# One sixteenth of the output weights loaded by GpSimd in six row transfers, with ten 2-byte transfers between them, in a fused decode block (attention and MLP) on one core

## The chip, the cores and the metric

One Trainium2 chip, one of its cores. The metric is the device time of one execution in microseconds (us), as a median over executions. The kernel before takes 669.44 us (four executions, 669.28 to 669.69). None was over 1.5% above the fastest of its kernel, and all count as fast. Faster or slower are given at 2%, 13.4 us.

## The reference

Eight sequences decode one token each through an attention layer with a key and value cache, and a two-layer MLP, both with conditional layer norms. Cut to what matters here:

```python
B, Sq, D = (8, 1, 512);  Hq, Hkv, Sk, Dh = (32, 8, 8192, 128);  F = 1792
h = layernorm(x) * (1 + ca) + sa
q = (h @ wq)                                   # 32 heads
scores = einsum(q, k_cache) * Dh ** -0.5       # the cache: 2 x 8 x 8 x 8192 x 128 bf16
o = einsum(softmax(scores), v_cache)
x = x + ga * (o @ wo)                          # wo: 4096 x 512 bf16, 4 MB
h = layernorm(x) * (1 + cb) + sb
x = x + gb * (relu(h @ w1 + b1) ** 2 @ w2 + b2)
```

The cache is 268 MB, all inputs together 284 MB. Each byte is used once.

## The kernel before

SyncE issues nearly all loads into a ring of four slots of 4 MB. The tiles of this kernel have up to 128 rows, called partitions (`[128, ...]` in its code). The parts that matter are the output weights `wo`, loaded once near the start, and their first reader near the end.

```python
wo_sb = sb("wo_sb", [128, HQ, D], BF16)
...
load(0)                      # keys of the first two heads, 4 MB, 32 KB per partition
load(1)
d_b1 = dma("sync", s_bb, ...)
d_b2 = dma("sync", s_bb, ...)
d_wo = dma("sync", s_wo, lambda e: e.dma_start(
    wo_sb[:, :, :].rearrange("p (g j) n -> p g (j n)", j=4),
    A_wo.rearrange("(g p j) n -> p g (j n)", g=8, p=128)))   # 8 groups x 128 rows of 4 KB
load(2)                      # waits until the slot is free, as do all later loads
load(3)
...
# last batch: the first reader of wo (24 matmuls), then 32 more for groups 6 and 7
t = op("tensor", lambda e, g=g, j=j: e.matmul(bank(7)[32 * j:32 * (j + 1), :], ...,
       wo_sb[:, 4 * g + j, :], ...), [k_oP, d_wo])
...
# last of all: the second MLP weight, the output, the store
```

Of the kernel before, what the change touches and what calls it, by code (L numbers as in the profile page):

```python
# [9 lines left out]
BF16 = mybir.dt.bfloat16  # L10
# [23 lines left out]
class Prog:  # L34
# [19 lines left out]
    def op(self, eng, fn, deps=()):  # L54
        o = Op(eng, fn, deps, None, self.at)
        o.tok = Tok(o, self.at)
        self.ops[eng].append(o)
        return o.tok

    def dma(self, eng, sem, fn, deps=()):  # L60
        self.dma_n[sem] = self.dma_n.get(sem, 0) + 16
        self.ops[eng].append(Op(eng, fn, deps, sem, self.at))
        return Tok(None, self.at, sem, self.dma_n[sem])
# [105 lines left out]
def bass_adaLN_cond__gqa_block_cached__dense_activation_squared_relu__decode_kernel(  # L169
# [17 lines left out]
    with ExitStack() as es:  # L187
        E = es.enter_context
        sb = lambda name, shape, dt: E(nc.sbuf_tensor(name, shape, dt))
        RING = sb("ring", [128, NSLOT, UNIT], BF16)  # L190
        KTb = sb("KTb", [128, 2, 32, 128], BF16)
        wo_sb = sb("wo_sb", [128, HQ, D], BF16)
# [24 lines left out]
        ONE8 = sb("ONE8", [1, B], BF16)  # L217
        PERM = sb("PERM", [128, 4, 32], BF16)
        epst = sb("epst", [128, 1], FP32)
        stats = sb("stats", [B, 6], FP32)  # L220
        mv = sb("mv", [B, 2], FP32)
        std_ = sb("std_", [B, 1], FP32)
# [47 lines left out]
        Pg = Prog(nc, E)  # L270
        op, dma = Pg.op, Pg.dma
        sem = lambda name: E(nc.semaphore(name))
        s_c, s_x, s_wm, s_wq, s_wo, s_bb = (
            sem(f"d_{n}") for n in ("c", "x", "wm", "wq", "wo", "bb"))
        s_w1 = [sem(f"d_w1{i}") for i in range(2)]
        s_w2 = [sem(f"d_w2{i}") for i in range(4)]
        s_ring = [sem(f"d_r{i}") for i in range(NSLOT)]
# [63 lines left out]
        k_all = t  # L341
# [9 lines left out]
        def load(n):  # L351
            kv, b, p = units[n]
            s = n % NSLOT
            src = (A_k_cache if kv == "k" else A_v_cache)[b, 2 * p:2 * p + 2]
            src = src.rearrange("g s d -> (g s d)").rearrange("(p f) -> p f", p=128)
            dep = [released.get(s)]
            if units[n] == last:
                t0, toks = 0, []
                for i, t1 in enumerate(CH):
                    toks.append(dma("sync", s_last[i], lambda e, a=t0 * DH, z=t1 * DH: e.dma_start(  # L360
                        RING[:, s, a:z], src[:, a:z]), dep))
                    t0 = t1
                loaded[n] = toks
            else:
                loaded[n] = dma("sync", s_ring[s], lambda e: e.dma_start(slot(s), src), dep)
# [67 lines left out]
        for g in range(HKV):  # L433
            r0 = 16 * (g % 2) + 4 * (g // 2)
# [3 lines left out]
        def fcol(ap, f):  # L438
# [9 lines left out]
        load(1)  # L448
        d_b1 = dma("sync", s_bb, lambda e: e.dma_start(b1_row, B_b1.rearrange("(o f) -> o f", o=1)))
        d_b2 = dma("sync", s_bb, lambda e: e.dma_start(b2_row, B_b2.rearrange("(o f) -> o f", o=1)))  # L450
        d_wo = dma("sync", s_wo, lambda e: e.dma_start(
            wo_sb[:, :, :].rearrange("p (g j) n -> p g (j n)", j=4),
            A_wo.rearrange("(g p j) n -> p g (j n)", g=8, p=128)))
        load(2)
        load(3)
        next_load = NSLOT
# [53 lines left out]
        def permute(q0, q1, dst, deps):  # L510
            pP = bank(6)[:, 64 * q0:64 * q1].rearrange("p (g j b) -> p g j b", j=4, b=B)
            for hl in range(REP):
                for j in range(4):
                    t = op("tensor", lambda e, hl=hl, j=j: e.matmul(
                        pP[32 * hl:32 * (hl + 1), :, j, :].rearrange("p (q h) b -> p h q b", h=2),
                        PERM[:, j, :], oTn_p[:, :, q0:q1, hl, :], start=True, stop=True,
                        tile_position=(0, 32 * hl)), deps)
            return op("vector", lambda e: e.tensor_copy(dst, pP), [t])

        def project(k_oP):  # L520
            for g in range(6):
                for j in range(4):
                    t = op("tensor", lambda e, g=g, j=j: e.matmul(
                        bank(7)[32 * j:32 * (j + 1), :], oP[:, g, :, :].rearrange("p j b -> p (j b)"),
                        wo_sb[:, 4 * g + j, :], start=(g == 0), stop=(g == 5), tile_position=(0, 32 * j)),
                        [k_oP, d_wo])
            return op("vector", lambda e: e.tensor_copy(proj, bank(7)), [t])

        for b in range(B):
# [5 lines left out]
            for p in range(NP):  # L535
                n = 2 * NP * b + p
# [69 lines left out]
            for p in range(NP):  # L606
                if p == NP - 1:
                    Pg.at = "post" if lastb else (b, "b")
                n = 2 * NP * b + NP + p
# [3 lines left out]
                if not lastu:  # L613
# [30 lines left out]
                    if lastb and p == NP - 2:  # L644
                        Pg.at = "post"
                        k_proj = project(permute(0, 3, oP[:, 0:6], [norm_last, k_all] + stg_free + hold))
                        for k in range(KT):
                            op("tensor", lambda e, k=k: e.matmul(
                                yT_ps[:, k, :], b2_row[:, k * 128:(k + 1) * 128], ONE8[:, :],
                                start=(k == 0), stop=False, skip_group_check=True), [d_b2, s_bank_free[2]])  # L650
                else:
# [22 lines left out]
                    for m in range(28):  # L674
# [6 lines left out]
                        if m == 15:  # L681
                            for f in range(FT):
                                op("tensor", lambda e, f=f: e.matmul(
                                    hT_ps[f // 7][:, f % 7, 1, :], fcol(b1_row, f), ONE8[:, :],
                                    start=(f % 7 == 0), stop=False, skip_group_check=True), [d_b2, s_bank_free[f // 7]])
                            for k in range(KT):
                                op("tensor", lambda e, k=k: e.matmul(
                                    attn_ps[:, k, :], proj[:, 128 * k:128 * (k + 1)], SELP[:, :],
                                    start=(k == 0), stop=False, skip_group_check=True), [k_proj])
                    osb = O_sb[:, 1, :]  # L690
                    t = op("vector", lambda e: e.tensor_copy(osb, bank(3)), [t])
                    for i in range(4):
                        op("tensor", lambda e, i=i: e.matmul(
                            oT_ps, osb[:, i * 128:(i + 1) * 128], SEL[:, i, :], start=(i == 0), stop=False,
                            skip_group_check=True), [t, k_all])
# [4 lines left out]
                    k_oP = permute(3, 4, oP[:, 6:8], [t])  # L700
                    for g in (6, 7):
                        for j in range(4):
                            for k in range(KT):
                                k_attn = op("tensor", lambda e, g=g, j=j, k=k: e.matmul(
                                    attn_ps[:, k, :], wo_sb[:, 4 * g + j, k * 128:(k + 1) * 128], oP[:, g, j, :],
                                    start=False, stop=(g == 7 and j == 3), skip_group_check=True), [k_oP, d_wo])


        t = op("vector", lambda e: e.tensor_tensor(t1T[:], attn_ps, mod(2), ALU.mult), [k_attn])
# [2 lines left out]
        for k in range(KT):  # L712
            t = op("tensor", lambda e, k=k: e.matmul(mean_ps, ONESMB[:, :], x1T[:, k, :], start=(k == 0),
                                                    stop=(k == KT - 1)), [k_x1])
        o_ps = bank(4)[:, 0:256]
        for cc in range(2):
            for k in range(2):
                op("tensor", lambda e, k=k, cc=cc: e.matmul(
                    o_ps[64 * cc:64 * cc + B, 128 * k:128 * (k + 1)], x1T[:, 2 * cc + k, :], IDENT[:, :],
                    start=(k == 0), stop=False, tile_position=(0, 64 * cc), skip_group_check=True), [k_x1])  # L720
# [10 lines left out]
        for k in range(KT):  # L731
# [4 lines left out]
            for f in range(FT):  # L736
                t = op("tensor", lambda e, f=f, k=k: e.matmul(
                    hT_ps[f // 7][:, f % 7, :, :], wcol(k, f), hbT[:, k, :, :], start=False, stop=(k == KT - 1),
                    skip_group_check=True), [k_hb, k_sb, d_w1[k // (KT - 1)]])
# [9 lines left out]
        for f in range(FT):  # L749
            for k in range(KT):  # L750
                t = op("tensor", lambda e, f=f, k=k: e.matmul(
                    yT_ps[:, k, :], W2v[:, f, k * 128:(k + 1) * 128], hidT[:, f, :],
                    start=False, stop=(f == FT - 1), skip_group_check=True), [k_sq[f // 7], d_w2[f // 4]])
# [3 lines left out]
        for cc in (1, 0):  # L757
            for k in range(2):
                t = op("tensor", lambda e, k=k, cc=cc: e.matmul(
                    o_ps[64 * cc:64 * cc + B, 128 * k:128 * (k + 1)], y2T[:, 2 * cc + k, :], IDENT[:, :],  # L760
                    start=False, stop=(k == 1), tile_position=(0, 64 * cc), skip_group_check=True), [k_y2])
# [39 lines left out]
```

## Time and profile before

| what | value | view |
|---|---|---|
| time | 669.44 us | four executions |
| span of the profiled execution | 667.6 us | page |
| bytes read | 283.66 MB, 425 GB/s over the span | page |
| share of the DMA engines' time on SyncE's queue (q1) | 99.1% | page |
| TensorE busy | 513.8 us, 77% | page |
| chain that ended last | PE 52%, DMA 37% | page |

The chain names TensorE for half of the span, since each key load is released by the TensorE work that empties its slot (SyncE's own waits: 342.4 us for the matmuls of L496, 31 times, and 215.9 us for those of L630, 28 times). The queue table shows the stronger limit: the 16 DMA engines are at work nearly all the time, 99.1% of it for SyncE's queue. SyncE's own timeline shows how its loads are issued at the start (start, length, engine, line, operation, tile, count):

```profile
3.68 0.40 SPq L451 DMA_DIRECT2D wo_sb<-in_A_wo_dram  x1
14.59 23.87 SPq L365 DMA_DIRECT2D ring<-in_A_k_cache_dram  x2
```

The third and fourth key loads are entered from 14.59 on; the second of them is not accepted before 38.46 (14.59 + 23.87).

### The profile page before, as it was taken

How to read it: one execution, taken by the hardware profiler on the slowest of the kernel's cores; microseconds unless marked ns; L12 is line 12 of the kernel's file. 1: busy time of each engine (PE TensorE's matmuls, PEld its weight loads, DVE VectorE, ACT ScalarE, POOL GpSimd, SP SyncE). 2: the span in 40 equal slices, each digit the busy share in tenths (PEclk: the TensorE clock that was granted, in tenths of full speed). 3: DMA queues.
4: the chain of work that ended last, by engine and by line, in shares of the span. 5: the costliest groups of instructions: out<-in, count | busy, mean ns of one | idle time of the engine just before them, and what ended most of it. 6: DMA issues, size and time to landing. Idle time of an engine off the chain costs nothing.

```text
span 667.6 us, 15485 instructions
## 1 busy us (share of the span) xinstructions
PE 513.8 (77%) x7064; PEld 344.8 (52%) x7064; DVE 302.6 (45%) x571; ACT 258.7 (39%) x289; POOL 18.4 (3%) x76
## 2 busy tenths in 40 slices
PE   3493984898739985699848987499756998389885
PEld 2283731675328742577317853287425773177534
DVE  2262731566216651367314662166513673156722
ACT  2151640466105660266404662066502654046610
POOL 7300000000000000000000000000000000000000
PEclk9696997899969998699977999699987999779996
DMA  9999999999999999999999999999999999999996
GB/s 376 431 412 437 426 427 435 432 430 430 434 434 430 430 432 436 428 432 432 436 428 430 434 434 430 430 434 434 428 432 434 434 426 434 432 434 428 434 415 264
DMA packets 12176, 283.85 MB, mean 425 GB/s; under 512 B 1250, under 2 KB 1283, under 8 KB 3588
## 3 DMA queue, kind: packets, MB, share of 16 engines
q1 hardware_dynamic: 12116, 283.65, 99.1%
q8 instruction: 9, 0.15, 0.1%
q10 hardware_dynamic: 48, 0.02, 0.0%
q14 instruction: 3, 0.02, 0.0%
HBM read 283.66 MB, written 0.01 MB: 425 GB/s over the span
## 4 chain that ended last, share of the span: by engine, by line
PE 52%; DMA 37%; ACT 7%; DVE 2%; SPq 1%; issue 1%
PE PS L479 36%; DMA ring<-in_A_k_cache_dram 32%; PE PS L496 9%; ACT P_sb L562 5%; PE PS L616 2%; DMA ring<-in_B_w_dram 2%; DMA ring<-in_A_wq_dram 2%; PE PS L469 1%; SPq L659 1%; ACT KTb L484 1%; DVE O_sb L626 1%; PE PS L463 1%; PE PS L574 1%; DVE Pm L588 0%; PE PS L594 0%
## 5 line engine op out<-in xcount | busy, mean ns | idle before, releaser
L484 ACT ACTIVATE KTb<-PS 128x1024 bf16<-128x1024 bf16 x192 | 196.5, 1024 | 332.2 <-PE PS L479 332.2
L479 PE MATMUL PS<-IDENT,ring 128*128 128x128 bf16 x4096 | 267.4, 227 | 51.2 <-DMA ring<-in_A_k_cache_dram 51.2
L479 PEld LDWEIGHTS PS<-IDENT,ring 128*128 128x128 bf16 x4096 | 246.8, 102 | 99.6 <-DMA ring<-in_A_k_cache_dram 52.4
L486 DVE COPY KTb<-PS 128x1024 bf16<-128x1024 bf16 x320 | 210.1, 687 | 143.9 <-PE PS L479 141.8
L616 PE MATMUL PS<-ring,Pm 128*32 128x512 bf16 x992 | 70.4, 434 | 46.8 <-DMA ring<-in_A_v_cache_dram 45.9
L496 PE MATMUL PS<-KTb,Qb 128*32 128x512 bf16 x1024 | 78.8, 385 | 4.5 <-ACT KTb L484 4.5
L626 DVE CAST O_sb<-PS 128x512 bf16<-128x512 f32 x31 | 21.4, 692 | 126.7 <-PE PS L616 126.7
L616 PEld LDWEIGHTS PS<-ring,Pm 128*32 128x32 bf16 x992 | 26.8, 106 | 85.5 <-DMA ring<-in_A_v_cache_dram 54.4
L562 ACT ACTIVATE P_sb<-PS,negm 128x1024 bf16<-128x1024 f32 x32 | 35.2, 1112 | 20.2 <-DVE negm L557 20.2
L469 PE MATMUL PS<-ONES 128*128 128x512 f32 x80 | 42.1, 630 | 0.0
L574 PE MATMUL PS<-IDENT,P_sb 128*128 128x128 bf16 x256 | 19.9, 220 | 15.4 <-ACT P_sb L562 15.4
L588 DVE COPY Pm<-PS 64x512 bf16<-64x512 bf16 x48 | 20.2, 421 | 25.0 <-PE PS L574 24.5
L574 PEld LDWEIGHTS PS<-IDENT,P_sb 128*128 128x128 bf16 x256 | 14.4, 98 | 25.1 <-ACT P_sb L562 25.1
L463 PE MATMUL PS<-IDENT 128*128 128x512 bf16 x88 | 26.9, 380 | 0.0
L496 PEld LDWEIGHTS PS<-KTb,Qb 128*32 128x32 bf16 x1024 | 15.4, 94 | 21.1 <-ACT KTb L484 8.5
L503 DVE TENSOR_REDUCE m<-PS 128x1 f32<-128x512 f32 x32 | 22.0, 689 | 6.6 <-PE PS L496 6.6
L630 PEld LDWEIGHTS PS<-SEL,O_sb 128*128 128x128 bf16 x124 | 5.8, 97 | 30.5 <-DVE O_sb L626 30.5
L469 PEld LDWEIGHTS PS<-ONES 128*128 128x128 f32 x80 | 12.7, 190 | 10.6 <-issue 10.6
L630 PE MATMUL PS<-SEL,O_sb 128*128 128x8 bf16 x124 | 7.9, 169 | 12.4 <-DVE O_sb L626 12.0
L641 DVE TENSOR_TENSOR oTn<-PS,rinv 128x8 f32 x31 | 6.0, 194 | 14.9 <-PE PS L630 14.9
L463 PEld LDWEIGHTS PS<-IDENT 128*128 128x128 bf16 x88 | 7.7, 105 | 9.1 <-issue 7.2
L484 ACT ACT_TABLE_LOAD x8 | 10.3, 1283 | 3.2 <-issue 3.2
(132 smaller groups left out, 115.9 us busy)
## 6 DMA issues: line engine op xcount, KB each, us to landing
ring<-in_A_k_cache_dram SPq DMA_DIRECT2D x32, 4096.0 KB, 34.2
ring<-in_A_v_cache_dram SPq DMA_DIRECT2D x31, 4096.0 KB, 27.8
ring<-in_A_wq_dram SPq DMA_DIRECT2D x1, 4096.0 KB, 19.9
wo_sb<-in_A_wo_dram SPq DMA_DIRECT2D x1, 4096.0 KB, 47.6
ring<-in_w_mod_dram SPq DMA_DIRECT2D x1, 3072.0 KB, 10.3
ring<-in_A_v_cache_dram SPq DMA_DIRECT2D x1, 2048.0 KB, 22.6
ring<-in_B_w_dram SPq DMA_DIRECT2D x3, 512.0 KB, 19.4
ring<-in_B_w_dram SPq DMA_DIRECT2D x1, 1344.0 KB, 17.9
```

The source lines that it names most:

```text
L463: ts = [op("tensor", lambda e: e.matmul(bank(at).rearrange("p (a r) -> p a r", a=4), IDENT[:, :], rhs)) for _ in range(n)]
L469: ts = [op("tensor", lambda e: e.matmul(bank(at).rearrange("p (a r) -> p a r", a=4), ONES[:, :], rhs)) for _ in range(n)]
L479: t = op("tensor", lambda e, j=j, i=i: e.matmul(STG[j][:, i, :], src[:, 32 * k + 8 * j + i, :], IDENT[:, :], is_transpose=True), [loaded[n ...
L484: stg_free[j] = op("scalar", lambda e, j=j, dst=dst: e.activation(dst, STG[j], ACT.Copy), [t])
L486: stg_free[j] = op("vector", lambda e, j=j, dst=dst: e.tensor_copy(dst, STG[j]), [t])
L496: t = op("tensor", lambda e, hf=hf, q=q, rhs=rhs: e.matmul(PS[32 * q:32 * (q + 1), k, :], Qb[:, 2 * p + hf, :], rhs, start=(p == 0 and hf ...
L503: return op("vector", lambda e: e.tensor_reduce(m4[:, k:k + 1], bank(k), AX.X, ALU.max), [t])
L562: exps.append(op("scalar", lambda e, k=k: e.activation(P_sb[:, k, :, :, :], bank(k).rearrange("p (i x) -> p i x", i=8).unsqueeze(2).to_bro ...
L574: t = op("tensor", lambda e, k=k, i=i: e.matmul(STG[k][:, i, :], P_sb[:, k, i, :, :].rearrange("p h x -> p (h x)"), IDENT[:, :], is_transp ...
L588: done.append(op("vector", lambda e, dst=dst, frm=frm: e.tensor_copy(dst, frm), [t, k_pm]))
L616: t = op("tensor", lambda e, p=p, m=m, cg=cg, vt=vt, Obank=Obank: e.matmul(Obank[32 * cg:32 * (cg + 1), :], lhs[:, p, 32 * m:32 * m + 32], ...
L626: t = op("vector", lambda e, osb=osb, Obank=Obank: e.tensor_copy(osb, Obank), [t])
```

## The change

The change takes columns 1024 to 2048 of the last group, 128 rows of 2 KB, off SyncE and gives them to GpSimd in transfers of 17, 19, 23, 23, 23 and 23 rows. Ten transfers of one element go around them: one before the first, five between, four after the last. The form of the code (a table of sixteen places, with a rotation that is set to 0) suggests that each row transfer was meant to use one chosen DMA engine of the sixteen, and the 2-byte transfers to step over the others. That is a reading of the code.

```diff
-        d_wo = dma("sync", s_wo, lambda e: e.dma_start(
-            wo_sb[:, :, :].rearrange("p (g j) n -> p g (j n)", j=4),
-            A_wo.rearrange("(g p j) n -> p g (j n)", g=8, p=128)))
+        wo_d = wo_sb[:, :, :].rearrange("p (g j) n -> p g (j n)", j=4)
+        wo_s = A_wo.rearrange("(g p j) n -> p g (j n)", g=8, p=128)
+        d_wo = [dma("sync", s_wo, lambda e: e.dma_start(wo_d[:, 0:7, :], wo_s[:, 0:7, :])),
+                dma("sync", s_wo, lambda e: e.dma_start(wo_d[:, 7, 0:1024], wo_s[:, 7, 0:1024]))]
+        r0 = 0
+        for i in range(16):
+            r1 = r0 + (0, 17, 0, 19, 0, 23, 0, 23, 0, 23, 0, 23, 0, 0, 0, 0)[(i + 0) % 16]
+            if r1 > r0:
+                d_wo.append(dma("gpsimd", s_wo2, lambda e, r0=r0, r1=r1: e.dma_start(
+                    wo_d[r0:r1, 7, 1024:2048], wo_s[r0:r1, 7, 1024:2048]), [k_all]))
+            else:
+                d_nil = dma("gpsimd", s_nil, lambda e, i=i: e.dma_start(nil[0:1, i:i + 1], A_wo[0:1, 0:1]), [k_all])
+            r0 = r1
+        d_wo = [d_wo[1], d_wo[-1]]
+        Pg.wait("gpsimd", [d_nil])
```

Left out of the diff: a 32-byte tile for the single elements, two semaphores, and the two readers of `wo`, which now wait for both semaphores.

More of the change, by code (lines that the diff above doesn't have):

```diff
@@ L219, in bass_adaLN_cond__gqa_block_cached__dense_activation_squared_relu__decode_kernel @@
         epst = sb("epst", [128, 1], FP32)
+        nil = sb("nil", [1, 16], BF16)
         stats = sb("stats", [B, 6], FP32)
@@ L272, in bass_adaLN_cond__gqa_block_cached__dense_activation_squared_relu__decode_kernel @@
         sem = lambda name: E(nc.semaphore(name))
-        s_c, s_x, s_wm, s_wq, s_wo, s_bb = (
-            sem(f"d_{n}") for n in ("c", "x", "wm", "wq", "wo", "bb"))
+        s_c, s_x, s_wm, s_wq, s_wo, s_bb, s_nil, s_wo2 = (
+            sem(f"d_{n}") for n in ("c", "x", "wm", "wq", "wo", "bb", "nil", "wo2"))
         s_w1 = [sem(f"d_w1{i}") for i in range(2)]
@@ L525, in project @@
                         wo_sb[:, 4 * g + j, :], start=(g == 0), stop=(g == 5), tile_position=(0, 32 * j)),
-                        [k_oP, d_wo])
+                        [k_oP] + d_wo)
             return op("vector", lambda e: e.tensor_copy(proj, bank(7)), [t])
@@ L705, in bass_adaLN_cond__gqa_block_cached__dense_activation_squared_relu__decode_kernel @@
                                     attn_ps[:, k, :], wo_sb[:, 4 * g + j, k * 128:(k + 1) * 128], oP[:, g, j, :],
-                                    start=False, stop=(g == 7 and j == 3), skip_group_check=True), [k_oP, d_wo])
+                                    start=False, stop=(g == 7 and j == 3), skip_group_check=True), [k_oP] + d_wo)
         t = op("vector", lambda e: e.tensor_tensor(t1T[:], attn_ps, mod(2), ALU.mult), [k_attn])
```

## The prediction

> **What bounds the kernel now.** I read the page's 40 slices first, then the DMA queues, then the chain that ended last, then short windows over the last microseconds, and last the timeline there. The slices and the queue table say that this kernel is a stream of bytes:
>
> ```profile
> DMA  9999999999999999999999999999999999999996
> GB/s 376 431 412 437 426 427 435 432 430 430 434 434 430 430 432 436 428 432 432 436 428 430 434 434 430 430 434 434 428 432 434 434 426 434 432 434 428 434 415 264
> ...
> q1 hardware_dynamic: 12116, 283.65, 99.1%
> q8 instruction: 9, 0.15, 0.1%
> ```
>
> The 16 DMA engines are busy in every slice, at about 431 GB/s, which is 26.9 GB/s for each. Nearly everything runs on one queue (q1, issued by SyncE). The other row to remember is q8: nine packets of 0.15 MB in total, 16 KB each, are instruction fetches[...].
>
> The transfer to be changed is this one of the list of issues, and it is long done before it is read:
>
> ```profile
> wo_sb<-in_A_wo_dram SPq DMA_DIRECT2D x1, 4096.0 KB, 47.6
> ```
>
> and in the view of this tile its readers are:
>
> ```profile
> L704 PE MATMUL PS<-KTb,wo_sb x32: 167/168/188, 656.0 to 656.8; 128*128 128x8 bf16 x32
> L523 PE MATMUL PS<-wo_sb,KTb x24: 379/379/390, 648.6 to 649.7; 128*32 128x512 bf16 x24
> ```
>
> It is issued at 3.7 us, lands 47.6 us later, at 51.3, and its first reader starts at 648.6. So its latency is worth nothing; only the bytes it puts on each engine count. The end of the run is what shows whose bytes count. The columns of the next view are the window, its length, busy time (and count) of PE, weight loads, VectorE, ScalarE and GpSimd, the granted clock, the DMA share and GB/s:
>
> ```profile
> 661.00:661.50 0.50, 0.00 (x0) 0.00 (x0) 0.43 (x3) 0.00 (x0) 0.00 (x0) 0.50 0.84 311
> 661.50:662.00 0.50, 0.32 (x12) 0.33 (x13) 0.46 (x3) 0.00 (x0) 0.00 (x0) 0.50 0.46 180
> 662.00:662.50 0.50, 0.50 (x25) 0.50 (x22) 0.22 (x1) 0.00 (x0) 0.00 (x0) 0.50 0.34 115
> 662.50:663.00 0.50, 0.20 (x8) 0.11 (x4) 0.00 (x0) 0.00 (x0) 0.00 (x0) 0.50 0.08 20
> 663.00:663.50 0.50, 0.00 (x0) 0.00 (x0) 0.00 (x0) 0.00 (x0) 0.00 (x0) 0.50 0.06 25
> 663.50:664.00 0.50, 0.43 (x16) 0.44 (x16) 0.00 (x0) 0.00 (x0) 0.00 (x0) 0.50 0.02 8
> ```
>
> One engine of 16 is a share of 0.06. So the engines do not finish together: about half are done by 661.75, some five are still at work at 662.25, and from about 662.7 to 663.7 one engine works alone. The trace's packet records name its trouble: a 16 KB instruction fetch begins 2.4 us before its last data packet[...]. I call it the late engine. The last two waits on the path are for it:
>
> ```profile
> 649.42 14.74 DMA ring<-in_B_w_dram
> 664.16 0.05 issue
> 664.21 0.39 PE PS L751 x8
> ```
>
> The last piece of the second MLP weight lands at 664.16; eight matmuls, a multiply, four transposing matmuls, a copy and the store follow, 3.4 us. **The end is set by the latest of sixteen engines, not by the mean.**
>
> [...]
>
> **The change, part by part.** The sizes come from the diff, the packet times from the packet records of the trace: a 4 KB packet takes 159 ns, a 2 KB packet 84 ns, and a row of them advances by 80 ns.
>
> *Removed from SyncE's queue:* columns 1024 to 2048 of the last group, 128 rows x 2048 B = 256 KB, 16 KB on each engine. Each engine's eight 4 KB packets become eight of 2 KB: 8 x (159 - 80) = 0.63 us less. This is time on all 16 engines, and since they have no gap, each of them should be 0.63 us earlier from then on.
>
> *Added on GpSimd's queue:* transfers of 17, 19, 23, 23, 23, 23 rows, 128 in all. [...] An engine with 23 rows pays 23 x 82 ns = 1.89 us, one with 19 1.56, one with 17 1.39. Net of the 0.63: **six engines become later by 0.8 to 1.3 us, ten earlier by 0.63.** The ten tiny packets take below 0.1 us each (a 4 B semaphore packet takes 9 ns, a 512 B packet 25 to 40)[...]: under 0.1 us.
>
> *SyncE:* one more issue, 404 ns by the row of the old one. It issues at 3.7 and then waits until 14.59. Off the path: 0.
>
> *GpSimd:* sixteen issues after its last select at 26.85. [...] It has no other work afterwards. Its last wait is for a few bytes[...]. Off the path: 0. While it works, TensorE waits for the third key load anyway, until 61.47 with 10.55 us idle[...].
>
> *TensorE:* one more semaphore to look at before line 523, long reached. [...]the path at that point is the DMA queue, not TensorE: 0.
>
> *The sum* depends on one fact, whether the late engine is one of the six:
> - Late engine not loaded: it ends 0.63 earlier. The five that ended about a microsecond before it may be loaded and come to -1.0 + 1.3 = 0.3 later than it does now, so -0.6 to +0.3, and -0.5 if the six were chosen with care. 669.57 - 0.5 = 669.1.
> - Late engine loaded: 0.8 to 1.3 later, 670.4 to 670.9.
> - [...]
>
> What could be gained in all is limited: in the last view TensorE is done with what has landed at 662.70, and the rest of its matmuls on this weight needs 1.0 us (line 751, 24 at 663.57). So with data in place it would be through at 663.7 in place of 664.6: a gain of more than about 0.9 us can't come from this.
>
> **The rivals.** (1) *Nothing at all shows* (the ends even out): engines catch up wherever the queue runs empty and all start again together. Against it: the DMA share is 0.97 to 1.06 in every 13 us window from 40 to 651, so no common pause in which a late engine would catch up is to be seen. It would make 669.6. (2) *The software path costs much more than its bytes:* [...]2 KB packets that wait a turn behind each 32 KB packet of the other queue (1.21 us). A row per turn is 23 x 1.3 = 30 us for one transfer. That would put the landings at 60 to 100 us, still 550 us too early to matter. For a loss of 2%, 13.4 us, the engines would have to stand still that long, with the share near 0 for most of one slice. I see nothing that would do it; it would make about 683. (3) *Another timing of instruction fetches:* the changed program of GpSimd and the shift of TensorE's stream could put the last 16 KB fetch on another engine or outside the last 3 us. That is worth up to [...]the one microsecond by which it trails: 668.9. (4) *A fixed cost of a queue that was idle before,* at the beginning or end of the program: before has no such transfer, so its profile cannot rule it out[...].
>
> **Range and chances.** I give the first case 0.5, the second 0.3, the third 0.2: 0.5 x 669.1 + 0.3 x 670.65 + 0.2 x 669.5 = 669.65. I say 669.6, which is no change. The range from 668.7 to 671.0 holds all three cases, with 0.3 for the rivals at the lower side and 0.1 above; the executions of one kernel lie within 0.4 us. 2% is 13.4 us, more than ten times what any case moves: 0.98 for within 2%, and 0.01 for each side.
>
> **What would show it.** In the profile after: q1 at 283.39 MB and a new queue of 0.26 MB; two wo transfers of 3584 and 256 KB from SyncE, six from GpSimd of 34 to 46 KB landing between 30 and 100 us; DMA share still near 1.0 in all windows to 651; the last MLP weight landing at 664.16 less 0.6 or plus up to 1.3; in the last windows a tail of one engine that is shorter (first case) or of up to six engines that is longer (second). The prediction would be wrong if slices in the first 100 us fell well under 430 GB/s, if TensorE or SyncE waited long for the new semaphore, or if the span grew before 651 while the share of the queues fell.

The sum came to 669.65, 0.5 x 669.1 + 0.3 x 670.65 + 0.2 x 669.5, and the forecast to 669.6. Its third term is the rows of a transfer spread over many engines, which came to 669.0 to 669.9, in the middle 669.5. The first two terms assume that each row transfer is on one engine and the six on different ones, as the form of the code suggests. No trace shows that. That the removed 256 KB were shared evenly by the 16 engines is an assumption of the estimate too.

## The result, and the profile after

670.93 us, the median of four executions (670.24 to 671.86), against 669.44: 1.49 us more. The ratio is 1.0023 with a 95% interval of 1.0005 to 1.004. Ratios are the mean time of one kernel's fast runs over that of the other's of the same rounds, so not quite the ratio of the medians quoted here. By the 2% rule the two are the same; the interval leaves out 1, so a loss of 0.05 to 0.4% is there. The profiled execution is the shortest of the four (670.24, span 668.4).

The page of the changed kernel, the GB/s of the 40 slices of 16.7 us and the queues:

```profile
GB/s 376 437 361 446 422 436 430 428 429 437 431 431 428 435 437 426 429 433 437 426 433 431 437 428 429 431 437 433 424 431 437 435 428 426 437 437 426 426 423 280
...
q1 hardware_dynamic: 12132, 283.39, 99.1%
q0 software_dynamic: 512, 0.26, 0.2%
```

The bytes moved to the new queue as they should. One slice stands out: the third, 361 GB/s in place of 412. Shorter windows place it. The columns are the window, its length, busy time and count of PE, weight loads, VectorE, ScalarE, GpSimd, then clock, DMA share and GB/s. Before:

```profile
39.00:46.00 7.00, 7.00 (x122) 5.69 (x120) 4.69 (x8) 4.09 (x4) 0.00 (x0) 1.00 0.99 393
46.00:55.00 9.00, 5.41 (x88) 3.86 (x88) 3.69 (x6) 4.09 (x4) 0.00 (x0) 1.00 1.07 444
```

and after:

```profile
39.00:46.00 7.00, 7.00 (x118) 5.41 (x116) 4.69 (x8) 4.23 (x5) 0.00 (x0) 1.00 0.99 318
46.00:55.00 9.00, 5.93 (x98) 4.27 (x95) 4.21 (x7) 4.33 (x5) 0.00 (x0) 1.00 1.08 439
```

From 39 to 46 us the engines moved 75 GB/s less, with the same share of busy time, 0.99. They did not stand idle: the packets took longer. The trace's packet records (start, duration, size and queue of each packet; the profile's sums are made of them) show the same: SyncE's 4 KB packets between 39.5 and 45 us took a median of 159 ns before and 198 ns after.

A finer measure comes from the same records: the time at which a given number of megabytes had moved (a packet's bytes spread evenly over its duration), after less before. I call it the **lag** of the stream.

| MB moved | 12 | 14 | 16 | 18 | 24 | 40 | 150 | 264 | 282 |
|---|---|---|---|---|---|---|---|---|---|
| time before, us | 30.43 | 35.10 | 39.86 | 44.74 | 58.92 | 96.14 | – | – | – |
| lag of the changed kernel, us | 0.05 | 0.18 | 0.29 | 1.39 | 1.48 | 1.48 | 1.48 | 1.48 | 1.48 |

The stream loses 1.4 us once, while the GpSimd transfers are under way, and carries the loss to the end without gaining or losing anything more. The median time rose by 1.49 us, about as much as the lag.

GpSimd's timeline of the changed kernel, in part:

```profile
27.17 0.68 POOL L463 DMA_DIRECT2D nil<-in_A_wo_dram  x1 [0.31 <-POOL PERM L310]
27.84 0.53 POOL L460 DMA_DIRECT2D wo_sb<-in_A_wo_dram  x1
28.36 0.51 POOL L463 DMA_DIRECT2D nil<-in_A_wo_dram  x1
```

An issue took GpSimd 0.51 to 0.53 us, the first one 0.68. Its list of issues (transfers, KB, median us to landing):

```profile
wo_sb<-in_A_wo_dram POOLq DMA_DIRECT2D x4, 46.0 KB, 12.1
nil<-in_A_wo_dram POOLq DMA_DIRECT2D x10, 0.0 KB, 11.5
```

The packet records say how the rows were dealt out. The new queue has 61 packets of 4096 B and 6 of 2052 B, besides small ones. Two rows are 4096 B, and a last odd row with 4 B behind it is 2052. A transfer of 17 rows in pairs makes 8 + 1 such packets, one of 19 makes 9 + 1, four of 23 make 4 x (11 + 1), together 61 + 6. The sizes alone do not say on how many engines they ran: the one transfer of 128 rows of e4 below has packets of 4096 B too. Two more records do. There are also 29 packets of 8 B, and 61 + 6 + 29 = 96 = 6 x 16, as if each transfer gave every engine either rows or an 8 B packet. And the packets of the first transfer (8 of 4096 B, one of 2052 B, seven of 8 B, from 33.97 to 34.78 us) overlap in time, up to five of the 4096 B ones at once. I read this as several engines, since the packets in flight on all queues are as many as the engines nearly all the time (16 in 94% of moments between 14 and 655 us, before and after). **So the rows went out two by two over several engines, not on one engine per transfer.** Which engines these were, and by what rule, the records do not tell.

SyncE's timeline after:

```profile
3.70 0.40 SPq L454 DMA_DIRECT2D wo_sb<-in_A_wo_dram  x1
4.14 27.92 SPq L455 DMA_DIRECT2D wo_sb<-in_A_wo_dram  x1
32.11 6.90 SPq L366 DMA_DIRECT2D ring<-in_A_k_cache_dram  x2
```

The second, small transfer of `wo` was held on SyncE for 27.9 us, and with it the third key load, which in the kernel before was entered at 14.59. That was a surprise, and one of the things to be tested. The chain that ended last shows it too: SyncE's part in it (SPq) was 1% before and is 6% now.

```profile
PE 52%; DMA 32%; ACT 7%; SPq 6%; DVE 2%; issue 1%
```

The last windows and the end of the chain, after:

```profile
663.00:663.50 0.50, 0.50 (x22) 0.50 (x23) 0.43 (x2) 0.00 (x0) 0.00 (x0) 0.50 0.47 180
663.50:664.00 0.50, 0.50 (x19) 0.43 (x17) 0.00 (x0) 0.00 (x0) 0.00 (x0) 0.50 0.29 98
664.00:664.50 0.50, 0.49 (x16) 0.41 (x16) 0.00 (x0) 0.00 (x0) 0.00 (x0) 0.50 0.07 16
664.50:665.00 0.50, 0.00 (x0) 0.00 (x0) 0.00 (x0) 0.00 (x0) 0.00 (x0) 0.50 0.00 0
```

```profile
650.25 14.73 DMA ring<-in_B_w_dram
664.98 0.05 issue
665.03 0.39 PE PS L764 x8
```

The engines finish closer together than before: the share goes from 0.47 to nothing within 1.5 us (663.0 to 664.5), where before it took two (661.5 to 663.7, at the end one engine alone). So this execution lost 1.48 us of stream and ended only 0.8 us later.

### The profile page after: what moved, and what is told of

Read it like the earlier page. It is cut to its first block, busy times and chain, and to the rows that moved or that the text cites. A ratio compares the mean times of both kernels' runs of the same rounds, so it can differ in the third digit from the quotient of the medians.

```text
span 668.4 us, 15503 instructions
## 1 busy us (share of the span) xinstructions
PE 514.6 (77%) x7064; PEld 344.7 (52%) x7064; DVE 302.6 (45%) x571; ACT 258.9 (39%) x289; POOL 26.7 (4%) x92
## 3 DMA queue, kind: packets, MB, share of 16 engines
q1 hardware_dynamic: 12132, 283.39, 99.1%
## 4 chain that ended last, share of the span: by engine, by line
PE 52%; DMA 32%; ACT 7%; SPq 6%; DVE 2%; issue 1%
PE PS L492 36%; DMA ring<-in_A_k_cache_dram 30%; PE PS L509 9%; ACT P_sb L575 5%; SPq L455 4%; PE PS L629 2%; DMA ring<-in_B_w_dram 2%; PE PS L482 1%; ACT KTb L497 1%; SPq L672 1%; DVE O_sb L639 1%; PE PS L476 1%; PE PS L587 1%; DVE Pm L601 0%; PE PS L607 0%
## 5 line engine op out<-in xcount | busy, mean ns | idle before, releaser
L497 ACT ACTIVATE KTb<-PS 128x1024 bf16<-128x1024 bf16 x192 | 196.7, 1024 | 332.7 <-PE PS L492 332.7
## 6 DMA issues: line engine op xcount, KB each, us to landing
ring<-in_A_v_cache_dram SPq DMA_DIRECT2D x31, 4096.0 KB, 27.9
```

What stands on the lines that cost most here:

```text
L497: stg_free[j] = op("scalar", lambda e, j=j, dst=dst: e.activation(dst, STG[j], ACT.Copy), [t])
```

## The experiments

All twelve were timed in five rounds, with the kernel before run on the same chip between them; its medians were 669.42 to 669.53. The comparison with the reference passed for all twelve. Of three of them (e10, e11, e12) rows of the last group are in wrong partitions on purpose; the contribution of `wo` to the output is small, and the comparison does not notice it. So it is no proof of those rows, in any of the runs.

The lag is read at 282 MB, against the profiled execution of the kernel before. It is one execution of each kernel, and how far it varies between executions was not measured; e2 and e3, which lose nothing, differ from zero by 0.01 and 0.04.

| run | the last 256 KB (or what differs) | lag, us | median, us | over before, us | ratio, 95% interval |
|---|---|---|---|---|---|
| the change | GpSimd, 6 row transfers + 10 of 2 B | 1.48 | 670.93 | +1.49 | 1.0005 to 1.004 |
| e1_no_nil | GpSimd, 6 row transfers | 1.59 | 670.70 | +1.28 | 1.0008 to 1.0035 |
| e2_nil_only | kernel before + 10 of 2 B | 0.01 | 669.61 | +0.19 | 0.9993 to 1.0021 |
| e3_sp_split | SyncE, 1 transfer of 128 rows | 0.04 | 669.41 | -0.01 | 0.9988 to 1.0015 |
| e4_one_sw | GpSimd, 1 transfer of 128 rows | 0.14 | 669.46 | +0.04 | 0.9988 to 1.0016 |
| e5_sw_cols | GpSimd, 4 transfers of 128 rows x 512 B | 0.60 | 669.73 | +0.25 | 0.9987 to 1.0014 |
| e6_sp_rows16 | SyncE, 8 transfers of 16 neighbouring rows | 1.29 | 670.78 | +1.30 | 1.0004 to 1.0031 |
| e7_sw_strided | GpSimd, 6 transfers, every sixth row | 0.97 | 669.90 | +0.42 | 0.9992 to 1.002 |
| e8_no_nil_late | as e1, issued after `wo` had landed | 2.16 | 671.06 | +1.58 | 1.0008 to 1.0035 |
| e9_near | SyncE, see below | 2.86 | 672.42 | +2.89 | 1.0029 to 1.0056 |
| e10_own | SyncE, see below | 2.34 | 671.98 | +2.45 | 1.0022 to 1.0049 |
| e11_sp_every4 | as e6, written to every fourth partition | 0.74 | 670.27 | +0.85 | 0.9998 to 1.0026 |
| e12_sp_every8 | as e6, written to every eighth partition | 1.34 | 671.22 | +1.80 | 1.0015 to 1.0042 |

### The parts of the change

**e1_no_nil.** Only the 2-byte transfers are taken away:

```diff
-            else:
-                d_nil = dma("gpsimd", s_nil, lambda e, i=i: e.dma_start(nil[0:1, i:i + 1], A_wo[0:1, 0:1]), [k_all])
-        Pg.wait("gpsimd", [d_nil])
```

> The change without its ten 2-byte transfers; the six GpSimd transfers stay. In the changed kernel the stream of bytes falls 1.43 us behind that of before between 31 and 46 us (packet records: time at which 24 MB had moved, 58.92 against 60.40 us) and stays behind to the end. Theory A (each small packet of the software queue costs its engine some 45 ns, and every GpSimd transfer brings about 28 small ones, whatever it carries): six transfers have 234 of the 512 packets, so the lag is about 0.65 us and the time 0.6 to 0.8 us over before. Theory B (data packets of two queues that take turns cost it; small packets are free): lag stays 1.4 us, time 1.5 us over before. [...]

Measured: the whole lag stays, 1.59 us, and the time with it, +1.28. The sizes of the data packets are the same, 61 and 6. Theory A, that each small packet costs, asked for 0.65 us; it falls. (It also counted wrongly: the queue table of this run has 192 packets on the software queue, not 234.) That the small transfers steer where the rows go (a theory C) finds no support in the packet sizes; the records do not number the engines, so which engines were used cannot be seen.

**e2_nil_only.** The kernel before, plus the ten 2-byte transfers:

```diff
+        for i in range(10):
+            d_nil = dma("gpsimd", s_nil, lambda e, i=i: e.dma_start(nil[0:1, i:i + 1], A_wo[0:1, 0:1]), [k_all])
+        Pg.wait("gpsimd", [d_nil])
```

> The kernel before, with ten 2-byte GpSimd transfers and nothing else; the output weights all from SyncE in one transfer. Theory A: ten transfers have about 280 small packets, lag 0.8 us, time 0.8 us over before, for 20 bytes. Theory B: lag 0 to 0.1 us, time as before.

Measured: lag 0.01 us, time +0.19 with an interval that holds 1. The queue table of this run shows that they did run:

```profile
q0 software_dynamic: 320, 0.00, 0.0%
```

320 packets, and nothing lost. Theory A falls for good.

**e3_sp_split.** The same three pieces, the third from SyncE too:

```diff
+                dma("sync", s_wo, lambda e: e.dma_start(wo_d[:, 7, 1024:2048], wo_s[:, 7, 1024:2048]))]
```

> The output weights in the same three pieces, the last 256 KB in one transfer from SyncE too; no GpSimd transfer. Theory A and B: lag below 0.1 us, time as before, though SyncE's second issue is held for some 28 us as in the changed kernel. Theory D (the loss comes from the split and from the held issue, which delays the later key loads): lag 1.4 us, time 1.5 us over before.

Measured: lag 0.04, time as before. SyncE's second issue was held as in the changed kernel (27.33 us from 4.19 on) and its third for 4.96 us. So neither the split nor the held issue costs anything: theory D falls, and the 6% of SyncE in the chain that ended last, which this run's page shows as well, is no cost. The engines had work meanwhile: their share in this run is 0.97 from 27 to 39 us, and 0.96 in the kernel before.

**e4_one_sw.** One GpSimd transfer in place of sixteen:

```diff
+        d_wo.append(dma("gpsimd", s_wo2, lambda e: e.dma_start(
+            wo_d[:, 7, 1024:2048], wo_s[:, 7, 1024:2048]), [k_all]))
```

> The 256 KB in one GpSimd transfer of 128 partitions, no 2-byte transfers. About 64 data packets of 4 KB and 28 small ones. Theory A: 92 packets, lag 0.26 us, time 0.2 to 0.3 us over before. Theory B: the data packets are as many as in the changed kernel, lag 1.4 us, time 1.5 us over before.

Measured: lag 0.14, time +0.04. It has 64 data packets of 4 KB on the software queue, as many as the changed kernel has, with the same bytes from the same issuer. Theory B, that packets of two queues that take turns cost, falls. It lands by 38.7 us, just as SyncE's 4 KB packets start (at 38.9 in the kernel before, at 39.2 in the changed one), so this leaves a doubt that e8 takes up. What is left is the shape and the number: six transfers of a few neighbouring rows.

### Why the shape costs

So I took up a theory E: a transfer of a few rows costs by which partitions it writes, and a transfer of all 128 partitions does not. The mechanism that I had for it is not shown by any trace or run. What the runs can test is the shape.

**e5_sw_cols.** Four GpSimd transfers, but each with all 128 partitions:

```diff
+        for c0 in range(1024, 2048, 256):
+            d_wo.append(dma("gpsimd", s_wo2, lambda e, c0=c0: e.dma_start(
+                wo_d[:, 7, c0:c0 + 256], wo_s[:, 7, c0:c0 + 256]), [k_all]))
```

> The first four runs felled theory A and B: ten 2-byte transfers alone cost no lag (0.00 us), the six row transfers alone cost all of it (1.6 us), and the same 256 KB in one GpSimd transfer of 128 partitions costs 0.15 us. [...] Here the 256 KB come from GpSimd in four transfers of all 128 partitions and 512 B each: several transfers[...]. E: lag 0.1 to 0.3 us, time within 0.4 us of before. Rival F (every GpSimd transfer with data costs some 0.25 us, whatever its shape): lag 1.0 us, time 1 us over before.

Measured: lag 0.60, time +0.25. The time is where E had it. The lag is between the two theories, twice E's upper bound. Four such transfers cost four times what one does (0.14), so the number of GpSimd transfers with data may count, at about 0.15 us each (an estimate, 0.60 / 4); that the pieces are only 512 B long may count as well. This run does not separate the two. If it is the number, six transfers would cost some 0.9 us (an estimate, 6 x 0.15), and only the rest of the 1.6 us of e1 would belong to the rows.

**e6_sp_rows16.** No GpSimd transfer at all; SyncE loads the same rows in eight transfers:

```diff
+        for r0 in range(0, 128, 16):
+            d_wo.append(dma("sync", s_wo2, lambda e, r0=r0: e.dma_start(
+                wo_d[r0:r0 + 16, 7, 1024:2048], wo_s[r0:r0 + 16, 7, 1024:2048])))
```

> No GpSimd transfer: the same 256 KB from SyncE in eight transfers of 16 neighbouring rows each. E: [...]it costs as much as from GpSimd or more: lag 1 to 2.5 us, time 1 to 2.5 us over before. Rival G (only the software queue costs): lag below 0.1 us, time as before.

Measured: lag 1.29, time +1.30, as with GpSimd. Rival G falls: **eight transfers of 16 neighbouring rows from SyncE cost as much as the six from GpSimd (+1.30 and +1.28 us), so the software queue is not needed for it.** The windows of this run show it at its place, 380 against 444 before:

```profile
46.00:55.00 9.00, 4.99 (x84) 3.82 (x80) 3.27 (x5) 3.70 (x4) 0.00 (x0) 0.94 1.08 380
```

**e7_sw_strided.** Six GpSimd transfers of every sixth row:

```diff
+        for r0 in range(6):
+            d_wo.append(dma("gpsimd", s_wo2, lambda e, r0=r0: e.dma_start(
+                wo_d[r0:128:6, 7, 1024:2048], wo_s[r0:128:6, 7, 1024:2048]), [k_all]))
```

> Six GpSimd transfers again, of 21 or 22 rows each[...], but every sixth row, so that the rows of one transfer lie all over the partitions. E: [...]lag 0.3 to 0.8 us. Rival H ([...]six transfers of rows cost by their number): lag 1.4 to 1.6 us as with neighbouring rows.

Measured: lag 0.97, between E and its rival H. Against e1 (1.59) the partitions seem to matter, but not as much as I had it; and 0.97 is about what six GpSimd transfers would cost by their number alone, by the estimate from e5.

**e8_no_nil_late.** As e1, but issued after SyncE's part of `wo` has landed:

```diff
-                    wo_d[r0:r1, 7, 1024:2048], wo_s[r0:r1, 7, 1024:2048]), [k_all]))
+                    wo_d[r0:r1, 7, 1024:2048], wo_s[r0:r1, 7, 1024:2048]), [k_all, d_wo[1]]))
```

> The six row transfers without the 2-byte ones, issued only when the output weights from SyncE have landed, at about 52 us, so that they run among the 32 KB packets of the key loads and not among 4 KB packets. E: lag again 1.2 to 1.7 us, only later, from some 52 us on. Rival I (the cost comes from packets of two queues that take turns at 4 KB each): lag below 0.4 us.

Measured: lag 2.16, more than E had, and all of it after 55 us. Among the 32 KB packets of the key loads the six transfers cost more, not less (2.16 against the 1.59 of e1), so rival I falls. The window from 55 to 73 us of this run:

```profile
55.00:73.00 18.00, 11.16 (x147) 9.08 (x148) 5.75 (x9) 4.95 (x5) 0.00 (x0) 0.72 1.00 380
```

and of the kernel before:

```profile
55.00:73.00 18.00, 11.52 (x161) 9.26 (x162) 6.63 (x10) 5.62 (x6) 0.00 (x0) 0.72 1.01 432
```

By the packet records a 32 KB packet that began between 52 and 73 us took 1.35 us in the mean here and 1.22 before. Packets of a queue that nobody changed took longer.

### The partition alone

**e9_near and e10_own.** Two kernels that differ in one index. Rows 0 to 63 of the last group go out from SyncE in sixteen transfers of eight rows, rows 64 to 127 in one. What is read, the sizes, the number and the order are the same; in e10 the eight rows are written to every fourth partition of a block of 32.

```diff
-                    wo_d[a:a + 8, 7, c0:c0 + 1024], wo_s[a:a + 8, 7, c0:c0 + 1024])))
+                    wo_d[b:b + 29:4, 7, c0:c0 + 1024], wo_s[a:a + 8, 7, c0:c0 + 1024])))
```

> All from SyncE, result correct. The last group of the output weights (512 KB) is cut: rows 64 to 127 in one transfer, rows 0 to 63 in sixteen transfers of eight neighbouring rows of 2 KB. [...] E[...]: lag 0.7 to 2 us, of which the part of the 64-row transfer is common with the next run. Rival K (reading neighbouring rows in device memory, or many small transfers, costs): lag the same as in the next run.

> As e9_near, the same number of transfers, the same rows read[...]; only the partitions written differ: every fourth one of a block of 32[...]. The rows then lie in wrong partitions: the result is wrong on purpose. E: lag at least 0.4 us below that of e9_near, 0 to 0.6 us. Rival K: lag as in e9_near within 0.1 us.

Measured: lags 2.86 and 2.34. The difference of 0.52 us is in the range that E gave, and rival K, which allowed 0.1, falls, as far as one execution of each can say: in time the two are not clearly apart (671.70 to 673.46 and 671.57 to 672.56). But e10 itself was to have 0 to 0.6 and has 2.34. Why sixteen transfers of eight rows beside a 64-row transfer cost so much even then is not shown, and stays open.

**e11_sp_every4 and e12_sp_every8.** So I repeated the test without those complications: e6, with only the partitions written changed.

```diff
-                wo_d[r0:r0 + 16, 7, 1024:2048], ...
+                wo_d[b:b + 61:4, 7, 1024:2048], ...     # e11: b = 64 * (i // 4) + i % 4
+                wo_d[i:i + 121:8, 7, 1024:2048], ...    # e12
```

> As e6_sp_rows16 (lag 1.3 us, 670.8 us): SyncE, eight transfers of 16 rows, the same rows read; only the partitions written differ: every fourth of a block of 64[...]. Wrong on purpose. E[...]: lag about half, 0.3 to 0.8 us. Rival K (many small transfers, or the reads, cost): lag 1.2 to 1.4 us.

> As e11_sp_every4 with every eighth partition[...]. Wrong on purpose. [...]lag between that of e11_sp_every4 and that of e6_sp_rows16, 0.8 to 1.3 us. Rival K: 1.2 to 1.4 us.

Measured: lag 0.74 for e11 and 1.34 for e12. The times agree: all five executions of e12 (670.64 to 671.70) lie above all five of e11 (670.01 to 670.61). The lag of e12 is 0.04 above the range given for E (0.8 to 1.3) and inside that of rival K; e11 decides between them. The window from 46 to 55 us shows the order too: 403 and 370 GB/s, against 430 in e3. e3:

```profile
46.00:55.00 9.00, 5.58 (x91) 3.94 (x88) 3.86 (x6) 4.10 (x4) 0.00 (x0) 1.00 1.05 430
```

e11:

```profile
46.00:55.00 9.00, 5.10 (x86) 3.82 (x80) 3.38 (x6) 3.81 (x4) 0.00 (x0) 0.96 1.08 403
```

e12:

```profile
46.00:55.00 9.00, 6.11 (x101) 4.45 (x98) 4.39 (x7) 4.50 (x5) 0.00 (x0) 1.00 1.07 370
```

The four runs from SyncE side by side:

| run | the last 256 KB: partitions that a transfer writes | lag, us |
|---|---|---|
| e3_sp_split | all 128, in one transfer | 0.04 |
| e11_sp_every4 | 16, every fourth of a block of 64 | 0.74 |
| e12_sp_every8 | 16, every eighth of 128 | 1.34 |
| e6_sp_rows16 | 16 neighbours | 1.29 |

The last three read the same rows in as many transfers of the same size; only the partitions differ, and the lag with them. Rival K is out (it asked for 1.2 to 1.4 in e11). Distance alone is not it either: every eighth partition costs no less than neighbours (1.34 and 1.29), every fourth about half (0.74). So it is shown that the partitions written decide, all else being equal; by what mechanism is not shown.

These figures do not carry over to the other runs. From e9 to e10 the lag falls by 0.52 us only, from 2.86. Of the GpSimd runs e7 has 0.97, e1 1.59 and e8 2.16, and e5, which writes all 128 partitions each time, still lost 0.60. So how the 1.5 us of the changed kernel divide between the partitions written and the number of GpSimd transfers stays open.

No version beats the kernel before. e3 and e4 equal it.

## Why the prediction was right or wrong, point by point

The forecast was 669.6 us in a range of 668.7 to 671.0, "the same" with 0.98. Measured are 670.93 us and the same. The range holds it by 0.07 us, and the middle was wrong: no change was forecast, and 1.49 us came. That the range holds it is luck: its upper part stood for a late engine that gets a whole row transfer (670.4 to 670.9) and for rival 4, a fixed cost of a new queue (its figure was a guess). Neither happened.

- **What bounds the kernel: right.** The loss of 1.48 us in the stream was carried for 600 us to the end unchanged, and the median rose by as much. Rival 1, that engines catch up, is refuted by the constant lag. Rival 4, a fixed cost of an idle queue, was not the cause: the same new queue costs nothing in e2 (lag 0.01) and 0.14 us in e4.
- **Where the rows go: the third case.** I gave it 0.2. The prediction's main line, one engine per row transfer, did not happen: the new queue has 61 packets of two rows, and up to five of the first transfer ran at once.
- **The step that failed is the term for the third case in the sum,** which came to 669.5. It counted what each engine has to send, at 80 ns for a row, as if nothing but the engine's own rows set that time. The runs put the whole stream's delay of 1.3 to 1.6 us in its place (1.29 in e6, 1.59 in e1): packets got longer (a median of 198 ns for SyncE's 4 KB, against 159), and which partitions a row transfer writes decides how much (e11 0.74, e12 1.34). For the changed kernel itself the number of GpSimd transfers may have a part in it (e5 lost 0.60 with four). Why the partitions matter is not shown.
- **The 2-byte transfers: right.** Below 0.1 us was said; e2 has 0.01 of lag.
- **SyncE off the path: right in what counts, wrong in the length.** 404 ns were allowed, 27.9 us were measured. e3, with the same wait, is at 669.41.
- **GpSimd off the path: right.** Its issues took 8.3 us (16 instructions from 27.17 to 35.5), and nothing waited for them. The row transfers landed in the median 8.8 to 12.1 us after issue, not after 30 and more: rival 2 had the size of the delay wrong and its harmlessness right. After the first (0.68) the issues ran at an even 0.51 to 0.53 us, while VectorE was busy for 2.3 of the 8.3 us.
- **TensorE's one more wait: right.** No wait for it appears at the readers of `wo`: the only idle time that their tile view lists before them, 2.0 us in four pieces, ends with VectorE.
- **The late engine.** That the last engine sets the end is supported by the profiled execution, which lost 1.48 us of stream and, with a shorter tail, 0.8 us of time. The last weight landed at 664.98, 0.8 later, where the prediction had a loaded late engine, but no longer tail came with it, so this agreement is luck too. That the instruction fetch of before sat on the late engine is inferred: it ends at 662.33, where the last chain of packets begins (662.32, with two 4 KB packets of 441 and 347 ns in place of 159); the records have no engine numbers. In four executions the changed kernel spread over 1.6 us and the kernel before over 0.4 (over 1.0 in all the later rounds together); whether this is the tail too is not shown, since only one execution was profiled. Rival 3 (instruction fetches) was not tested.
- **What would show it** held partly: 283.39 MB and 0.26 MB on two queues, and landings of the row transfers from 30 us on, were as written. One of its signs of being wrong came as well: the third slice fell from 412 to 361 GB/s. "DMA share still near 1.0" held, but was no proof that nothing was lost: the share adds up the time of the packets, and the packets had become longer. GB/s of the same window was the column to watch.

## What to carry to other kernels

Where the DMA engines are busy all the time, try a load by all 128 partitions at once first, also when the piece is small: here 256 KB in one transfer cost nothing from SyncE and 0.04 us from GpSimd (lag 0.04 and 0.14), and the same bytes in six or eight transfers of a few neighbouring rows 1.3 us from either. A busy share near 1.0 did not show the loss (0.99 at 393 GB/s and at 318), so compare GB/s, or the time at which a given number of bytes has moved, between two traces. The time that this stream lost at one place was kept to the end (1.48 us from 24 MB to 282 MB).
